# Values and scores of two pairs in one visit of TensorE, and other PSUM banks for the scores

## The chip, the cores and the metric

One NeuronCore of a Trainium2 chip runs the kernel. The metric is the device time of one launch in microseconds, the median of several runs. PE is TensorE's matrix multiplication and PEld its weight load, DVE is VectorE, ACT is ScalarE, POOL is GpSimd, and SP is the engine whose queue issues the DMAs.

## What is computed

Attention with fixed sparsity, and then a two-layer feed-forward block on its output, all in float32:

```
scores = q @ k.T / sqrt(64)                  # 8 batches, 8 heads, 576 positions, 64 wide
heads 0 to 3: key within 32 positions behind the query
heads 4 to 7: key at the same place modulo 32, not after the query
attn = softmax(masked scores);  x = (attn @ v) as 4608 tokens of 512
h = x @ w_in;  g = h * sigmoid(1.702 * h);  out = g @ w_out      # 512 -> 2048 -> 512
```

## The kernel before

**Pairs.** The sparse attention is cut into 42 units that the code calls pairs. Each gathers a few query blocks with the few keys they see: "l" for the local heads, "s" for the strided ones. A pair p goes through these stages, each on its own engine:

- `scores(p)` (L222): small float32 products of 64 rows by 64 columns on PE, into two PSUM banks. A float32 product is two instructions in the trace, so 16 products show as 32.
- `maxima(p)` (L249): DVE adds the mask while it copies the two banks into the buffer `pr` (two SCALAR_TENSOR_TENSOR), then takes the row maxima (`nmax`).
- `softmax(p)` (L282): a generator; ACT makes eight exponentials, two to a step of the generator, then `rinv`; DVE takes its RECIPROCAL; POOL multiplies `pr` by it.
- `transpose(p)` (L309): DVE turns `pr` into `pt_l` or `pt_s` in four steps.
- `values(p)` (L362): PE multiplies `pt` with `v` into two banks `sa`, in 32 products for an "l" pair and 16 for an "s" pair; ACT copies the banks into the token tiles `xl`, `xs`; for the first token blocks DVE then makes a low half (`xl_1`, `xs_1`) from the same banks.

`attend(p)` (L754) is scores, the load of `qk` for pair p+2, maxima, and the start of softmax. Pairs 0 to 4 are done ahead of everything else; the other 37 are laid between the products of the feed-forward block.

**Feed-forward.** The tokens are nine blocks of 512. Every float32 operand is split into a high and a low half (float32r), and a product is three matmuls: high with high, high with low, low with high. Three stages follow each other:

- *Steps.* For blocks 0 to 2, 48 steps of one (block, f): `ffn1(s)` is 12 matmuls of 512 columns into a bank `h`; `act(s)` (L541) is a tanh on ACT and a SCALAR_TENSOR_TENSOR on DVE, both on that bank; `split(s)` makes the halves `gh` (ACT) and `gl` (DVE); `ffn2(s-2)` is 12 matmuls into four banks `o` that stay open for 16 steps. In the first 16 steps the weights are also made ready: per step two items, each two ACT operations on `raw` (`begin_word`, L503), a join on DVE (`raw<-raw`), a high half on ACT (`high`, L481, CAST `w<-raw`) and a low half on DVE (`low`, L493, `w<-raw,w`). The loop is at L981; trace step 9 runs from about 80.8 to 87.5 us.
- *Cycles.* For blocks 3 to 8, two blocks together, eight cycles for each of three rounds (`cycle`, L890): seven products of six matmuls each (a Winograd scheme: a11, s2, a12, s3, a22, s1, s4, banks `ha` and `hs`), and after product i `GAPS[i]` matmuls of the second layer from a queue (`fill`, L847).
- *Tails.* Behind each round of cycles, 16 groups of 12 second-layer matmuls.

**Order.** All engines keep the written order: each queue is first in, first out. The work of pairs is placed by three tables: `turn[p]` is the step in which pair p is transposed, `begin[p]` (L702) the step at whose end its scores are made, and `turn[p] + 2` the step of its values. For the five pairs 5 to 9 (`apart`, L360) `begin` was `turn - 3`; for later pairs it is `turn` of the pair two before, plus 2 or 3.

**Banks.** PSUM has eight banks, shared out by the first letter of a tile's name (L115):

```
def bank(name):
    tag, n = ("s", 2) if name[0] == "s" else ("x", 6)
```

So scores (`s0`, `s1`) and values (`sa0`, `sa1`) take turns in one couple of banks; the six others hold the four `o` and two for `h`, `ha` or `hs`. In a cycle the values of pair p stand in gap 6 (`valued_apart`), and the scores of pair p+2 in gap 0 of the next cycle (`owed`, `attend_ahead`), between two second-layer matmuls each. In the steps the values of pair 10 and later stand between `ffn1(s)` and `ffn2(s-2)`, and the scores of pair p+2 behind that `ffn2`.

Of the kernel before, what the change touches and what calls it, by code (L numbers as in the profile page):

```python
# [42 lines left out]
NF = DFF // P  # L43
# [10 lines left out]
AHEAD = 2  # L54
# [18 lines left out]
}  # L73
GAPS = (4, 4, 4, 3, 3, 3, 3)

# [27 lines left out]
def attn_ffn(ctx, tc, lqk, sqk, lv, sv, w_in, w_out, masks, out):  # L103
# [11 lines left out]
    def bank(name):  # L115
        tag, n = ("s", 2) if name[0] == "s" else ("x", 6)
        return psum.tile([P, 512], F32, tag=tag, name=name, bufs=n)
# [104 lines left out]
    def scores(p):  # L222

        nk, mask = geom(p)
        onto = p < n0
        sps = first[p % 2] if onto else [bank(f"s{j}_{p}") for j in range(2)]
        n = mask.shape[1]
# [119 lines left out]

    xs = {}

    def x_tiles(kind, j):  # L350
# [6 lines left out]
    def x_of(j, c):  # L357
        return (t[:, c % 2, :] for t in x_tiles("l" if c < 2 else "s", j))

    apart = range(n0, n0 + len(windows[0]))  # L360

# [338 lines left out]
    plain = range(n0, p)  # L700
    turn[p] = len(steps) + 2
    begin = {p: turn[p] - 3 for p in turn}  # L702
    for p in turn:
        if p - AHEAD in turn and p not in apart:
            begin[p] = turn[p - AHEAD] + (3 if p - AHEAD in apart else 2)
# [173 lines left out]

    def valued_apart(p):  # L880
        run(values(p))
        load_v(p + 2)

    def attend_ahead(p):
        if p + AHEAD < len(pairs):
            attend(p + AHEAD)

    owed = []

    def cycle(d, c, p, after, start, early):  # L890
# [18 lines left out]
        for i, k in enumerate(order):  # L909
# [47 lines left out]
            if i == 5:  # L957
                eased(HU)
            fill(GAPS[i] // 2)
            if i == 0 and owed:  # L960
                attend_ahead(owed.pop())
            if i == 6 and p is not None:
                valued_apart(p)
                owed.append(p)
            fill(GAPS[i] - GAPS[i] // 2)
        filling.extend(second(a, f + i, (a, f + i)) for i in range(2))
# [14 lines left out]
    for s in range(2, len(steps)):  # L981
# [17 lines left out]
        for k in now:  # L999
            low(k)  # L1000
        for p, t in turn.items():
            if t + 2 == s and p not in apart:
                run(values(p))
                load_v(p + 2)
        act(s)
# [5 lines left out]
        for p, t in turn.items():  # L1011
            if begin[p] < s < t:
                n = t - 1 - begin[p]
                i = s - begin[p]
                run(soft[p], 4 * i // n - 4 * (i - 1) // n)
            if t == s:
                turning[p] = transpose(p)
            if t <= s <= t + 1:
                run(turning[p], 2)
        if s >= LAG and s != NF:  # L1020
            ffn2(s - LAG)
        for p in apart:
            if turn[p] + 2 == s:
                run(values(p))
                load_v(p + 2)
        for p in turn:
            if begin[p] == s:
                attend(p)
        ahead(s)
# [4 lines left out]
    p = plain[-1] + 1  # L1034
    owed.append(plain[-1])
    s1, u2, v5, z = spare
# [7 lines left out]
    for d, (a, b) in enumerate(DOUBLES):  # L1044
# [10 lines left out]
        for c in range(NF // 2):  # L1055
            at = p if 1 <= c <= count else None
            after = p if at is None else p + 1
            after = after if after in soft or at is not None and after < len(pairs) else None
            rest = cycle(d, c, at, after, start, load_gate if c == NF // 2 - 1 else None)
            p += at is not None  # L1060
            start = rest
# [9 lines left out]
        for i in range(NF + 2 if outer else NF):  # L1071
# [3 lines left out]
            for k, q in enumerate(more):  # L1075
# [10 lines left out]
                if at == 3:  # L1086
                    valued_apart(q)
            if not outer:
                prepare(d + 1, i)
            fill(3 * NT)  # L1090
            if i == 0 and owed:
                attend_ahead(owed.pop())
            for k, q in enumerate(more):
                if i - 5 * k - 2 == 3:
                    attend_ahead(q)
        if not outer:
# [101 lines left out]
```

## Time and profile before

| what | value |
| --- | --- |
| median of 3 runs | 866.19 us (865.63 to 867.12) |
| the profiled execution's own time | 867.51 us |
| its span, first to last instruction | 865.7 us |
| PE busy | 853.1 us, 6538 matmuls |
| PEld busy | 682.8 us |
| DVE busy | 556.0 us |
| ACT busy | 440.2 us |
| POOL busy | 200.1 us |
| chain that ended last | PE 88%, DVE 5%, ACT 4% |

Busy shares are means over the whole span. The opening, the steps, the cycles and the tails differ, so what bounds the kernel is read stage by stage, and for PE from the distance between the starts of matmuls, since a busy PE is not yet a PE at its highest rate.

### The profile page before, as it was taken

To read this page: it belongs to the slowest core of one execution; us is meant where nothing else is said; L and a number is where in the kernel's file an instruction comes from. 1 tells how busy PE (TensorE), PEld (TensorE's weight loads), DVE (VectorE), ACT (ScalarE), POOL (GpSimd) and SP (SyncE) were. 2 spreads that over 40 slices of the span, in tenths; PEclk is the share of its full clock that TensorE was granted. 3 is DMA by queue.
4 is the path that set the end of the run, shared out by engine and by line. 5 is a ranking of instruction groups with operands and counts; after the bars stand their busy time and mean duration, and the time that the engine had idled before them with its cause. 6 is when DMAs were issued, how large, how long until landed. Compare 5 with 4: busy or idle time off the path is not lost.

```text
span 865.7 us, 17374 instructions
## 1 busy us (share of the span) xinstructions
PE 853.1 (99%) x6538; PEld 682.8 (79%) x6538; DVE 556.0 (64%) x989; ACT 440.2 (51%) x1330; POOL 200.1 (23%) x177
## 2 busy tenths in 40 slices
PE   9899999999999999999999999999999999999998
PEld 5687778778778877888878778878888888888886
DVE  3789986675576877577668776666766554444522
ACT  6798876544446544545445654545434433332321
POOL 3100104410054600423322012233240012232200
PEclk9999999999999999999999999999999999999999
DMA  9765323882254445676667536666555245455432
GB/s 335 304 243 200 133 64 124 265 258 94 80 168 155 136 141 167 213 211 191 183 189 240 183 116 201 186 182 197 169 160 184 73 161 169 149 166 147 145 123 73
DMA packets 76163, 148.86 MB, mean 172 GB/s; under 512 B 8240, under 2 KB 22960, under 8 KB 76080
## 3 DMA queue, kind: packets, MB, share of 16 engines
q1 hardware_dynamic: 76080, 147.76, 53.3%
q8 instruction: 52, 0.85, 0.4%
q14 instruction: 31, 0.25, 0.1%
HBM read 111.03 MB, written 36.70 MB: 171 GB/s over the span
## 4 chain that ended last, share of the span: by engine, by line
PE 88%; DVE 5%; ACT 4%; DMA 1%; issue 1%; SPq 0%; DVEq 0%; ACTq 0%
PE o L140 43%; PE hs L140 15%; PE h L140 12%; PE ha L140 11%; PE sa L140 3%; PE s L140 3%; DVE raw L140 1%; ACT pr L140 1%; ACT raw L140 1%; DVE w L140 1%; PE t L140 1%; ACT w L140 1%; DVE pt_l L140 1%; DMA raw<-w_out 1%; DVE pt_s L140 1%
## 5 line engine op out<-in xcount | busy, mean ns | idle before, releaser
L140 PE MATMUL o<-w,gh 128*128 128x512 f32 x1152 | 365.7, 393 | 0.3 <-DVE w L140 0.2
L140 PEld LDWEIGHTS o<-w,gh 128*128 128x128 f32 x1152 | 214.6, 188 | 45.5 <-DVE w L140 0.5
L140 PE MATMUL o<-w,gl 128*128 128x512 f32 x576 | 225.6, 392 | 0.0
L140 POOL TENSOR_TENSOR gl<-y,gh 128x512 fp32r<-128x512 f32 x45 | 59.8, 1328 | 301.1 <-ACT gh L140 142.2
L140 PEld LDWEIGHTS o<-w,gl 128*128 128x128 f32 x576 | 108.1, 188 | 22.8
L140 DVE SCALAR_TENSOR_TENSOR y<-tanh,y 128x512 f32<-128x512 f32 x96 | 70.3, 732 | 69.4 <-ACT tanh L140 66.0
L140 POOL TENSOR_TENSOR pr<-pr,rinv 128x432 f32<-128x432 f32 (+1 forms) x42 | 50.1, 1193 | 266.5 <-DVE rinv L140 266.5
L140 ACT ACTIVATE pr<-pr,nmax 128x54 f32<-128x54 f32 (+1 forms) x296 | 101.1, 346 | 5.1 <-DVE nmax L140 4.7
L140 ACT ACTIVATE tanh<-y 128x512 f32<-128x512 f32 x96 | 60.8, 633 | 79.1 <-DVE y L140 78.5
L140 PE MATMUL h<-xl,w 128*128 128x512 f32 x288 | 77.5, 403 | 1.9 <-ACT w L140 1.2
L140 PE MATMUL h<-xs,w 128*128 128x512 f32 x288 | 73.8, 391 | 0.0
L140 DVE TENSOR_TENSOR spare<-hs,spare 128x512 f32<-128x512 f32 x69 | 47.6, 690 | 38.2 <-PE hs L140 37.6
L140 DVE TENSOR_TENSOR gl<-spare,gh 128x512 fp32r<-128x512 f32 x48 | 33.2, 691 | 52.4 <-ACT gh L140 52.1
L140 PEld LDWEIGHTS h<-xl,w 128*128 128x128 f32 x288 | 51.6, 188 | 15.7 <-DVE w L140 2.7
L140 ACT CAST gh<-spare 128x512 fp32r<-128x512 f32 x48 | 29.9, 622 | 65.8 <-PE o L140 63.7
L140 PEld LDWEIGHTS h<-xs,w 128*128 128x128 f32 x288 | 53.8, 188 | 12.0 <-DVE w L140 0.4
L140 DVE STREAM_TRANSPOSE pt_l<-pr 32x256 f32<-32x256 f32 x128 | 55.7, 435 | 2.6 <-POOL pr L140 0.3
L140 DVE SCALAR_TENSOR_TENSOR g<-g,h 128x512 f32<-128x512 f32 x48 | 32.9, 685 | 36.6 <-ACT g L140 36.2
L140 ACT ACTIVATION_READ_ACCUMULATOR pr<-pr,nmax 128x1 f32 x296 | 56.2, 190 | 0.0
L140 DVE STREAM_TRANSPOSE pt_s<-pr 32x256 f32<-32x256 f32 x126 | 54.8, 435 | 2.0
L140 ACT ACTIVATE g<-h 128x512 f32<-128x512 f32 x48 | 29.1, 607 | 51.7 <-PE h L140 32.8
L140 POOL TENSOR_TENSOR y<-spare,spare 128x512 f32<-128x512 f32 x24 | 38.7, 1614 | 30.9 <-issue 28.0
(128 smaller groups left out, 1219.9 us busy)
## 6 DMA issues: line engine op xcount, KB each, us to landing
stream<-s SPq DMA_DIRECT2D x96, 256.0 KB, 2.7
stream<-a SPq DMA_DIRECT2D x72, 256.0 KB, 2.7
gate<-y SPq DMA_DIRECT2D x48, 256.0 KB, 2.3
spare<-gate SPq DMA_DIRECT2D x48, 256.0 KB, 2.8
qk<-sqk SPq DMA_DIRECT2D x23, 452.0 KB, 3.9
qk<-lqk SPq DMA_DIRECT2D x18, 576.0 KB, 4.1
v<-lv SPq DMA_DIRECT2D x18, 512.0 KB, 4.1
out<-out SPq DMA_DIRECT2D x36, 256.0 KB, 2.6
```

What stands on the lines that cost most here:

```text
L140: ins = call(*args, **kw)
```

## The change

Values of pair p and scores of pair p+2 are issued by one function, `visit`: first the value products, then the score products, the load of `qk`, the maxima, and then the copies of the values. Scores of pairs 12 and later get names with "c", which puts them into the six shared banks instead of the couple that the values use; pairs up to 11 keep the couple.

```
-GAPS = (4, 4, 4, 3, 3, 3, 3)
+GAPS = (4, 3, 3, 3, 3, 3, 5)
+FIRST = 1
...
-        sps = first[p % 2] if onto else [bank(f"s{j}_{p}") for j in range(2)]
+        sps = first[p % 2] if onto else [bank(f"{'s' if p - AHEAD in apart or p in apart else 'c'}{j}_{p}") for j in range(2)]
...
     for p in turn:
-        if p - AHEAD in turn and p not in apart:
+        if p - AHEAD in turn:
             begin[p] = turn[p - AHEAD] + (3 if p - AHEAD in apart else 2)
...
+    def visit(before, then):
+        rest = [(p, values(p)) for p in before]
+        for _, x in rest:
+            run(x, 1)
+        for p in then:
+            attend(p)
+        for p, x in rest:
+            run(x)
+            load_v(p + 2)
```

In a cycle the visit stands in gap 6 behind one second-layer matmul, and four follow it:

```
-            fill(GAPS[i] // 2)
-            if i == 0 and owed:
-                attend_ahead(owed.pop())
+            first = FIRST if i == 6 else 0
+            fill(first)
             if i == 6 and p is not None:
-                valued_apart(p)
-                owed.append(p)
-            fill(GAPS[i] - GAPS[i] // 2)
+                seen_to(p)
+            fill(GAPS[i] - first)
```

In a step the visit stands inside `ffn2(s-2)`: behind all of it in the first 16 steps, behind 8 of its 12 matmuls afterwards. The first half of the transposes of a pair (`t == s`) is now issued behind the visit, and it stood ahead of `ffn2` before:

```
+            if t + 1 == s:
+                run(turning[p], 2)
+        behind = second(*steps[s - LAG], s - LAG) if s >= LAG and s != NF else iter(())
+        run(behind, 2 * NT if s > NF else 3 * NT + 1)
+        visit([p for p in turn if turn[p] + 2 == s], [p for p in turn if begin[p] == s])
+        run(behind, 2 * NT)
+        for p, t in turn.items():
             if t == s:
                 turning[p] = transpose(p)
-            if t <= s <= t + 1:
                 run(turning[p], 2)
```

In the tails the scores follow the values without the 12 matmuls that lay between them. By the new `begin`, pairs 7, 8 and 9 have their scores in steps 8, 10 and 12 instead of 6, 8 and 10, one step ahead of their `turn` (9, 11 and 13).

Three places in the order of instructions are shown, before and now.

PE in a cycle, from the last value product of pair 27 on (`sa` is values, `s` and `c` scores of pair 29, `o` second layer, `ha` the product a11). Before:

```order
L140 MATMUL sa_27_4768<-pt_s,v_4408 64x54
L140 MATMUL o_3_4311<-w_1_913,gh_5_4665 128x512
L140 MATMUL o_3_4311<-w_1_913,gl_5_4666 128x512
L140 MATMUL ha_0_4_4793<-b11h,stream_4009 128x512 x4
L140 MATMUL ha_0_4_4793<-b11l,stream_4009 128x512 x2
L140 MATMUL o_0_4262<-w_1_996,gh_6_4708 128x512 x2
L140 MATMUL s_29_4808<-qk_4445 64x54
L140 MATMUL s_29_4809<-qk_4445 64x54
```

Now, where the rows left out are 13 more of the same two kinds of `c_29`:

```order
L141 MATMUL sa_27_4766<-pt_s,v_4430 64x54
L141 MATMUL c_29_4783<-qk_4420 64x54
...
L141 MATMUL c_29_4783<-qk_4420 64x54
L141 MATMUL c_29_4784<-qk_4420 64x54
L141 MATMUL o_2_4291<-w_1_913,gl_5_4666 128x512
L141 MATMUL o_3_4311<-w_1_913,gh_5_4665 128x512 x2
L141 MATMUL o_3_4311<-w_1_913,gl_5_4666 128x512
L141 MATMUL ha_0_4_4817<-b11h,stream_4009 128x512 x4
```

The ten matmuls of 512 columns between values and scores are gone from there, and four stand between the scores and a11.

ACT from step 8 into step 9 (`gh` is the half of step 8's activation, `pr` exponentials, `w` high halves of weights, `g` the tanh of step 9, `xl` the copies of the values of pair 6). Before:

```order
L140 CAST gh_1157<-g_8_1091 128x512
L140 ACTIVATE rinv_1161<-ssum_1015 128x8
L140 CAST w_0_1165<-raw_860 128x512
L140 CAST w_1_1167<-raw_863 128x512
L140 ACTIVATE g_9_1175<-h_1142 128x512
L140 ACTIVATE raw_916<-raw_916 128x512 x2
L140 ACTIVATE raw_919<-raw_919 128x512 x2
L140 ACTIVATE pr_97,ssum_1185<-pr_97,nmax_1138 128x96 x4
L140 CAST xl_0_1236<-sa_6_1202 128x2x4x32
```

Now:

```order
L141 CAST gh_1124<-g_8_1062 128x512
L141 ACTIVATE pr_98,ssum_1128<-pr_98,nmax_1105 128x54 x8
L141 ACTIVATE rinv_1137<-ssum_1128 128x8
L141 CAST w_0_1141<-raw_860 128x512
L141 CAST w_1_1143<-raw_863 128x512
L141 ACTIVATE g_9_1151<-h_1109 128x512
L141 ACTIVATE raw_916<-raw_916 128x512 x2
L141 ACTIVATE raw_919<-raw_919 128x512 x2
L141 CAST xl_0_1204<-sa_6_1170 128x2x4x32
```

All eight exponentials of pair 7 stand ahead of the high halves of the weights, and four of pair 8 are gone from behind the `raw` operations.

DVE at the same place, from the reciprocal on (`w` low halves, `g` step 9's activation, `pt_s` transposes of pair 7, `xl_1` low halves of the values of pair 6, the last row the join of step 10). Before:

```order
L140 RECIPROCAL rinv_1161<-rinv_1161 128x8
L140 TENSOR_TENSOR w_0_1165<-raw_860,w_0_1165 128x512
L140 TENSOR_TENSOR w_1_1167<-raw_863,w_1_1167 128x512
L140 SCALAR_TENSOR_TENSOR g_9_1175<-g_9_1175,h_1142 128x512
L140 STREAM_TRANSPOSE pt_s<-pr_98 32x8x32 x3
L140 TENSOR_TENSOR xl_1_1237<-sa_6_1202,xl_0_1236 128x2x4x32
L140 TENSOR_TENSOR xl_1_1237<-sa_6_1203,xl_0_1236 128x2x4x32
L140 SCALAR_TENSOR_TENSOR raw_916<-raw_916 128x512
```

Now:

```order
L141 RECIPROCAL rinv_1137<-rinv_1137 128x8
L141 TENSOR_TENSOR w_0_1141<-raw_860,w_0_1141 128x512
L141 TENSOR_TENSOR w_1_1143<-raw_863,w_1_1143 128x512
L141 SCALAR_TENSOR_TENSOR g_9_1151<-g_9_1151,h_1109 128x512
L141 TENSOR_TENSOR xl_1_1205<-sa_6_1170,xl_0_1204 128x2x4x32
L141 TENSOR_TENSOR xl_1_1205<-sa_6_1171,xl_0_1204 128x2x4x32
L141 STREAM_TRANSPOSE pt_s<-pr_98 32x8x32 x3
L141 SCALAR_TENSOR_TENSOR raw_916<-raw_916 128x512
```

The low halves of the values now stand ahead of the transposes. The reciprocal stands where it did, but what it waits for on ACT is now eight exponentials and not `rinv` alone.

## Rows read from the trace of the kernel before

**Rows 1.** The page: busy time, share of the span and instructions of each engine.

```profile
PE 853.1 (99%) x6538; PEld 682.8 (79%) x6538; DVE 556.0 (64%) x989; ACT 440.2 (51%) x1330; POOL 200.1 (23%) x177
```

**Rows 2.** Windows: us, busy by engine, granted clock, DMA share, GB/s.

```profile
96.00:106.00 10.00, 10.00 (x74) 7.80 (x73) 9.75 (x19) 9.73 (x33) 1.74 (x1) 1.00 0.30 106
106.00:116.00 10.00, 8.70 (x96) 6.47 (x95) 8.72 (x19) 7.14 (x20) 0.83 (x1) 1.00 0.01 2
130.00:330.00 200.00, 200.00 (x1906) 159.33 (x1906) 136.57 (x262) 102.26 (x386) 63.49 (x63) 1.00 0.49 161
```

**Rows 3.** Waits, 60 to 130 us: us in total, times, longest.

```profile
DVE xl L140 <- ACT xl L140: 1.3, 2, 0.8
PE h L140 <- ACT w L140: 1.2, 2, 1.0
PE h L140 <- DVE w L140: 0.7, 2, 0.3
```

**Rows 4.** Timeline of PE around a visit: start, us, engine, line, operation, tiles, count.

```profile
430.26 0.62 PE L140 MATMUL hs<-b22h,stream 128*128 128x512 f32 x2
430.72 0.61 PE L140 MATMUL hs<-b22l,stream 128*128 128x512 f32 x2
431.17 0.39 PE L140 MATMUL o<-w,gh 128*128 128x512 f32 x1
431.49 0.69 PE L140 MATMUL sa<-pt_s,v 54*64 54x54 f32 x32
432.10 0.50 PE L140 MATMUL o<-w,gh 128*128 128x512 f32 x1
432.44 0.40 PE L140 MATMUL o<-w,gl 128*128 128x512 f32 x1
```

**Rows 5.** The tile sa: durations in ns, least, median, most.

```profile
L140 PE MATMUL sa<-pt_s,v x672: 218/218/258, 73.7 to 632.5; 54*64 54x54 f32 x168
```

**Rows 6.** Timeline of DVE behind s4 of the same cycle.

```profile
431.37 0.69 DVE L140 TENSOR_TENSOR y<-hs,spare 128x512 f32<-128x512 f32 x1 [0.64 <-PE hs L140]
```

**Rows 7.** Timelines of PE and DVE around step 26: second layer, activation.

```profile
194.80 0.62 PE L140 MATMUL o<-w,gh 128*128 128x512 f32 x2
...
195.62 0.69 DVE L140 SCALAR_TENSOR_TENSOR g<-g,h 128x512 f32<-128x512 f32 x1 [1.62 <-ACT g L140]
```

**Rows 8.** Timelines of PE and DVE around the scores of step 19.

```profile
152.70 0.69 PE L140 MATMUL s<-qk 64*64 64x54 f32 x32
...
153.44 0.67 DVE L140 SCALAR_TENSOR_TENSOR pr<-s,masks_sb 128x216 f32<-128x216 f32 x2 [0.39 <-PE s L140]
```

**Rows 9.** Timeline of ACT, steps 8 to 10.

```profile
83.02 0.33 ACT L140 ACTIVATE pr<-pr,nmax 128x54 f32<-128x54 f32 x1
...
83.34 0.33 ACT L140 ACTIVATE pr<-pr,nmax 128x54 f32<-128x54 f32 x1
...
86.25 1.28 ACT L140 CAST w<-raw 128x512 fp32r<-128x512 f32 x2 [1.54 <-DVE raw L140]
87.51 0.60 ACT L140 ACTIVATE g<-h 128x512 f32<-128x512 f32 x1
88.00 2.35 ACT L140 ACTIVATE raw<-raw 128x512 uint32<-128x512 uint8 x4
...
90.61 0.36 ACT L140 ACTIVATE pr<-pr,nmax 128x96 f32<-128x96 f32 x1
...
91.69 0.61 ACT L140 CAST xl<-sa 128x256 fp32r<-128x256 f32 x2
```

**Rows 10.** Timeline of DVE, steps 8 to 10.

```profile
85.53 1.28 DVE L140 SCALAR_TENSOR_TENSOR raw<-raw 128x512 uint32<-128x512 uint32 x2
...
87.33 0.20 DVE L140 RECIPROCAL rinv<-rinv 128x8 f32<-128x8 f32 x1
...
89.33 0.68 DVE L140 SCALAR_TENSOR_TENSOR g<-g,h 128x512 f32<-128x512 f32 x1
...
92.07 0.76 DVE L140 TENSOR_TENSOR xl<-sa,xl 128x256 fp32r<-128x256 f32 x2 [0.82 <-ACT xl L140]
```

**Rows 11.** Timeline of PE, the opening.

```profile
1.00 2.74 PE L140 MATMUL t<-zeros 128*128 128x512 bf16 x6 [1.00 <-DVE zeros L140]
```

More of the change, by code (lines that the diff above doesn't have):

```diff
@@ L348, in attn_ffn @@
     xs = {}
+    apart = range(n0, n0 + len(windows[0]))
     def x_tiles(kind, j):
@@ L358, in x_of @@
         return (t[:, c % 2, :] for t in x_tiles("l" if c < 2 else "s", j))
-    apart = range(n0, n0 + len(windows[0]))
     def values(p):
@@ L700, in attn_ffn @@
     plain = range(n0, p)
-    turn[p] = len(steps) + 2
+    for i in range(AHEAD):
+        turn[p + i] = len(steps) + 2 + 2 * i
     begin = {p: turn[p] - 3 for p in turn}
     for p in turn:
-        if p - AHEAD in turn and p not in apart:
+        if p - AHEAD in turn:
             begin[p] = turn[p - AHEAD] + (3 if p - AHEAD in apart else 2)
@@ L878, in add, with seen_to @@
         vector.tensor_tensor(out=out, in0=a, in1=b, op=ALU.add)
[L880 to L888, printed above, removed]
+    def visit(before, then):
[7 more added lines that the diff above has]
+            load_v(p + 2)
+    def seen_to(p):
+        visit([p], [p + AHEAD] if p + AHEAD < len(pairs) else [])
     def cycle(d, c, p, after, start, early):
@@ L1000, in attn_ffn @@
             low(k)
[L1001 to L1004, printed above, removed]
         act(s)
@@ L1015, in attn_ffn @@
                 run(soft[p], 4 * i // n - 4 * (i - 1) // n)
+            if t + 1 == s:
[5 more added lines that the diff above has]
+        for p, t in turn.items():
             if t == s:
                 turning[p] = transpose(p)
-            if t <= s <= t + 1:
                 run(turning[p], 2)
[L1020 to L1028, printed above, removed]
         ahead(s)
@@ L1034, in attn_ffn @@
     p = plain[-1] + 1
-    owed.append(plain[-1])
     s1, u2, v5, z = spare
@@ L1057, in attn_ffn @@
             after = p if at is None else p + 1
-            after = after if after in soft or at is not None and after < len(pairs) else None
+            after = after if after in soft else None
             rest = cycle(d, c, at, after, start, load_gate if c == NF // 2 - 1 else None)
@@ L1086, in attn_ffn @@
                 if at == 3:
-                    valued_apart(q)
+                    seen_to(q)
             if not outer:
@@ L1090, in attn_ffn @@
             fill(3 * NT)
[L1091 to L1095, printed above, removed]
         if not outer:
```

## Prediction

> **What bounds the kernel now.** I read the page first: PE is busy 853.1 of 865.7 us [rows 1]. Busy is not peak rate, so the next view is PE's timeline. From 430.26 to 431.17 four matmuls of 512 columns start [rows 4], one in 0.227 us, and this is the distance nearly everywhere outside the small products. The windows then give the stages. From 130 to 330 us PE is busy 200.00 of 200 us at a granted clock of 1.00 [rows 2]: it waits for nothing, so whatever PE itself issues there is on the path. From 96 to 106 us DVE is busy 9.75 and ACT 9.73 of 10, and from 106 to 116 PE only 8.70 [rows 2]. The waits say for what: products h wait for weight halves, 1.2 us for ACT's and 0.7 for DVE's [rows 3]. So there are two bounds. Up to some 130 us, where weights are made ready, the pair of ACT and DVE sets the pace; behind that PE does.
>
> **The merged visits (gain).** What does leaving the wide matmuls for small ones cost? Around values of an "s" pair, second-layer matmuls start at 431.17 and 432.44 with one more and 32 small ones between [rows 4]. Without the small ones that would be two distances, 0.455 us; the visit costs 1.27 - 0.455 = 0.82. The 32 are busy 0.69 and the last of them lasts 0.22 [rows 5], so their starts spread over 0.47, and with one more distance of 0.015 they use 0.48. The other 0.335 is the change from wide to small and back: 0.09 on entry (431.49 - 431.17 - 0.227), 0.11 on the second wide matmul (432.44 - 432.10 - 0.227), the rest between the last small and the first wide one. Scores are of the same form, 64*64 [rows 8], and as busy, 0.69, so I take the same entry and exit for them. The change puts 30 scores, those of pairs 12 to 41, straight behind the values of pairs 10 to 39: 30 entries and exits go, 30 x 0.335 = 10.05 us, all beyond 130 us and on PE's path. No row shows values and scores side by side. The bounds are 0, if the junction costs as much as an exit and an entry, and 10.05, if it costs nothing. I take 10.05: inside a visit the products already change their operands and banks every 0.015 us.
>
> The Trainium skill, "TensorEngine Tiling (Array Packing)", section "Tiling Modes", Key Properties, says that TensorE is drained when the tiling mode changes and not when only the tile does. Values and scores both work in tiles of 64 by 64, so by it the junction is free; no row here shows that.
>
> **Waits of the scores for their new banks (loss).** One of the two banks was the last to be read. In a cycle that reader is DVE's add behind s4, from 431.37 to 432.06 [rows 6]. The scores would come 0.47 + 0.015 behind the first value product at 431.49, at 431.98, so they wait some 0.15 us with the signal's way. Values of an "l" pair have twice the instructions and cover it. Of the 12 merged visits in cycles 5 have "s" values: 0.75 us. In a step the reader is the activation: DVE ends it at 196.31, 1.51 us behind the first second-layer matmul [rows 7], and the scores come 8 x 0.227 + 0.09 + 0.485 = 2.39 behind it. Nothing, except in a step in which ACT also rounds a sum of weights (seven steps), say 0.35 in all (estimate). Together 1.1; bounds 0 and 3.
>
> **Waits for the score banks (nothing).** The next wide product needs the bank that DVE empties first. The scores' last start is at 152.70 + 0.47 = 153.17, DVE begins at 153.44 and two copies take 0.67 [rows 8], so the first is done some 0.6 us behind that start. Four second-layer matmuls lie between, 0.13 + 0.11 + 4 x 0.227 = 1.15 us. If that cover were gone, each visit would pay up to 0.6. For the wide "l" scores, if the product took the other bank, it would wait 0.1 to 0.2 in some dozen visits: this is in the upper bound of 3.
>
> **Gaps, queues.** After s2 and a12 one second-layer matmul less follows, after s4 two more. A product's bank is used again two products later, at least 12 starts or 2.7 us on; the reader needs 0.69 and begins within 0.64 us of DVE's wait [rows 6]. Nothing; without that cover 0.23 a piece. On SP the loads of `qk` and `v` now stand together behind a visit instead of half a step apart; each is for two pairs later, over 10 us on. Nothing.
>
> **The early stage (loss).** Here DVE and ACT are full, and the change puts one behind the other. Pairs 7, 8 and 9 get their scores one step before their transposes, so in steps 9, 11 and 13 all eight exponentials stand between the maxima and the high halves of the weights. One takes 0.32 us at width 54 (83.02 to 83.34), 0.36 at width 96 (90.61 to 91.69 is three) [rows 9]: 2.6 or 2.9 us. With 0.1 to start and 0.2 for `rinv`, DVE reaches the reciprocal 2.9 or 3.2 us after the maxima; before it, DVE has 1.8 us of joins and halves (85.53 to 87.33 [rows 10]). It idles 1.1, 1.4 and 1.1. Then its low halves wait for a high half of 0.65 that started with the reciprocal (pair of them 1.28 [rows 9]): 0.35 each. Sum 4.65.
>
> In the same steps DVE's low halves of the values now stand ahead of the transposes, and wait for ACT's copies, which stand behind 2.25 us of `raw` operations (88.00 to 90.25, overlap counted) and take 0.37 for the first. Before, the transposes filled that time. Against the activation's end (89.33 + 0.68 [rows 10]) carried along with the new delays, the wait is 1.2 in step 9, 0.4 in step 11 and 1.7 in step 13: 3.3. Before it was 1.3 in all [rows 3, 10], which goes. So DVE loses 4.65 + 3.3 - 1.3 = 6.7 us, and as PE already waits for these halves [rows 3], PE loses it too; nothing later gives it back, since PE is at its full rate there. Bounds: 3, if the maxima that leave the way (pair 8's, 2.0 us, and pair 9's, 1.3) give DVE a lead that holds; 10, if each copy wait is its full 1.8 and no idle time of before falls away.
>
> **Sum.** -10.05 + 1.1 + 6.7 = -2.25 us. Against the profiled execution's own 867.5 us (span 865.7) that is 865.3. The median of the runs shown, 866.2, lies 1.3 below that execution; the forecast for the median is **863.9 us**.
>
> **Rivals.**
> *A, the early stage hardly suffers.* DVE's lead holds and the stage loses 3: -10.05 + 1.1 + 3 = -5.95, 860.2 us. For it: DVE's maxima move two steps later. Against: DVE has no idle time in which to build a lead [rows 2].
> *B, the junction is not free.* Scores are other operands with other waits than values, so an entry and exit may remain in part. Half of it is 5.0 us: -5.0 + 1.1 + 6.7 = +2.8, 869.0 us, slower. It decides the sign from (10.05 - 7.8) / 30 = 0.075 us a junction. For it: nothing in the trace shows such a junction. Against: 0.015 us from product to product inside a visit.
> *C, TensorE's clock falls.* In steps 11 and 13 PE would stand still for about 2.4 us each time before h. In this trace the longest such wait is 1.0 [rows 3] and the granted clock stays at 1.00 [rows 2], so it shows no fall. At the lower level six wide matmuls took 2.74 us in the opening, about 0.45 each [rows 11], 0.22 more than now; a dozen of them after each hole are 2 x 2.7 = 5.4 us: +3.1, 869.3 us. The Trainium skill, "TensorE: Matmul & The Clock Gate", section "HAM oscillation — how this bites in real kernels", has the rule that a TensorE left idle between bursts is set back to half rate; no run here shows it for holes of this size.
> *D, no net change.* The junction or the bank waits take 2 us more than in the sum: within 0.2%.
>
> **From cases to numbers.** My forecast, both large terms within about 2 us of the sum, has 0.52. A has 0.20, B 0.10, C 0.05, D 0.13. A measurement of this kernel tells 0.2% from no change, 1.7 us. The forecast's own spread, 861.5 to 866, lies beyond 864.5 for a bit over six parts in ten: 0.33 of its 0.52 is faster and 0.19 the same. Faster: 0.33 + 0.20 + 0.02 of D = 0.55. Same: 0.19 + 0.08 of D = 0.27. Slower: B, C and 0.03 of D = 0.18. The range 859.5 to 868 leaves out the lower half of A and most of B and C, some 0.2; the forecast's own is 861.5 to 866.
>
> **What would show it.** Right: beyond 130 us visits of values and scores with starts 0.02 us apart at the junction, and a merged visit 0.33 us cheaper than the two; in cycles 0.1 to 0.2 of wait at the first scores behind "s" values; the stage up to h of step 16 some 6 to 7 us later, with DVE idle before the reciprocals and before the low halves of the values, and PE waiting over 2 us for ACT's or DVE's w in steps 11 and 13. Wrong: a gap at the junction; PE waits for score banks; a granted clock below 1.00; or an early stage that is hardly longer.

## The result, and the profile of the changed kernel

The changed kernel takes 871.68 us, the median of 7 runs (870.86 to 873.36), against 866.19 us of 7 runs of the kernel before (865.63 to 869.57): the ratio of the means is 1.0059, 95% interval 1.0045 to 1.0074. It is 0.6% slower. The forecast, 863.9 us with a range of 859.5 to 868, was wrong in size and in sign.

The profiled execution took 871.68 us itself (span 869.9). Its page, to be read against [rows 1]:

```profile
PE 851.6 (98%) x6538; PEld 690.9 (79%) x6538; DVE 557.0 (64%) x989; ACT 440.5 (51%) x1330; POOL 200.4 (23%) x177
...
PEclk9899899999999999999999999999999999999999
```

TensorE (PE) is busy 1.5 us less in a span 4.2 us longer, and in two of the forty slices the granted clock is under nine tenths of full, where it was above that in all forty before. The windows of [rows 2], now:

```profile
96.00:106.00 10.00, 7.64 (x59) 5.71 (x60) 8.00 (x14) 8.10 (x27) 1.47 (x1) 0.97 0.16 48
106.00:116.00 10.00, 10.00 (x68) 7.92 (x67) 8.40 (x19) 6.28 (x15) 0.00 (x0) 0.86 0.38 127
130.00:330.00 200.00, 196.14 (x1894) 158.97 (x1894) 136.24 (x262) 104.87 (x389) 62.82 (x63) 0.99 0.48 153
```

VectorE (DVE) and ScalarE (ACT), nearly full from 96 to 106 us before, now stand idle there a fifth of the time, and from 130 to 330 us TensorE, which never stopped before, lacks 3.9 us. The waits from 60 to 130 us say for what the first part waits, against [rows 3]:

```profile
PE h L141 <- ACT w L141: 4.2, 3, 1.6
DVE rinv L141 <- ACT rinv L141: 4.1, 3, 1.5
...
DVE xl L141 <- ACT xl L141: 2.8, 2, 1.7
DVE w L141 <- ACT w L141: 2.5, 5, 0.7
...
PE h L141 <- DVE w L141: 2.3, 3, 1.1
...
```

To find where the 4.2 us came in, the span is cut at four starts in TensorE's timeline: the first product of h in step 3, that of step 16, and the first product behind the steps (`ha`). In the kernel before they are:

```profile
44.33 1.65 PE L140 MATMUL h<-xl,w 128*128 128x512 f32 x6
...
131.89 1.52 PE L140 MATMUL h<-xl,w 128*128 128x512 f32 x6
...
332.65 0.84 PE L140 MATMUL ha<-b11h,stream 128*128 128x512 f32 x3
```

And in the changed one:

```profile
42.94 1.65 PE L141 MATMUL h<-xl,w 128*128 128x512 f32 x6
...
139.99 0.84 PE L141 MATMUL h<-xl,w 128*128 128x512 f32 x3
...
342.93 0.85 PE L141 MATMUL ha<-b11h,stream 128*128 128x512 f32 x3
```

The fourth cut is the start of the last matmul, 861.40 before and 865.62 now. So the opening is 1.39 us shorter, the **early stage** (step 3 to step 16) 97.05 us in place of 87.56 (+9.49), the **steps** from 16 on 202.94 in place of 200.76 (+2.18), and the **cycles** and what follows 522.69 in place of 528.75 (-6.06): +4.22 together. The opening differs from execution to execution (its end lay between 42.0 and 46.4 us over all profiles of this study, those with the order of before included), and the early stage does not depend on it: it took 97.05 us after openings that ended at 42.94, 44.23 and 44.52 us. So the stretches are compared, and the opening is left out.

Two merged visits show what the change gained. Around 488 us nothing waits:

```profile
488.24 0.39 PE L141 MATMUL o<-w,gl 128*128 128x512 f32 x1
488.56 0.69 PE L141 MATMUL sa<-pt_s,v 54*64 54x54 f32 x32
489.06 0.65 PE L141 MATMUL c<-qk 64*64 64x54 f32 x32
489.64 0.73 PE L141 MATMUL o<-w,gh 128*128 128x512 f32 x2
490.21 0.39 PE L141 MATMUL o<-w,gl 128*128 128x512 f32 x1
```

The scores `c` start 0.50 us behind the values, of which 31 distances of 0.015 are 0.47: the junction costs 0.03. From 488.24 to 490.21 is 1.97 us, less three wide distances of 0.227 it is 1.29, where two separate visits cost 1.64 [rows 4]: 0.35 is saved. In the cycles with "s" values the scores wait for DVE's add, as forecast:

```profile
405.48 0.69 PE L141 MATMUL sa<-pt_s,v 54*64 54x54 f32 x32
405.98 0.80 PE L141 MATMUL c<-qk 64*64 64x54 f32 x32
406.71 0.50 PE L141 MATMUL o<-w,gl 128*128 128x512 f32 x1
```

From the first value to the next wide matmul it is 1.23 us here and 1.08 above: 0.15 of wait, in five cycles. The loss in the steps is another matter. Step 41, first on TensorE:

```profile
297.66 0.61 PE L141 MATMUL o<-w,gh 128*128 128x512 f32 x2
...
299.56 1.14 PE L141 MATMUL sa<-pt_l,v 64*64 64x32 f32 x64
300.52 0.29 PE L141 MATMUL c<-qk 64*64 64x54 f32 x2
302.93 0.77 PE L141 MATMUL c<-qk 64*64 64x54 f32 x30 [2.12 <-DVE g L141]
303.63 0.80 PE L141 MATMUL o<-w,gl 128*128 128x512 f32 x1
```

The scores have two of the six shared banks. The first is free, the second is still read by the activation of the same step, and the visit stops for 2.4 us (300.54 to 302.93). ACT and DVE in that time:

```profile
294.36 0.60 ACT L141 ACTIVATE g<-h 128x512 f32<-128x512 f32 x1 [4.28 <-DVE gl L141]
294.85 0.33 ACT L141 ACTIVATE pr<-pr,nmax 128x54 f32<-128x54 f32 x1
...
297.44 1.03 ACT L141 CAST b11h<-xl 128x1024 fp32r<-128x1024 f32 x1
298.38 1.05 ACT L141 CAST plain<-summed 128x1024 fp32r<-128x1024 f32 x1
299.33 0.61 ACT L141 CAST gh<-g 128x512 fp32r<-128x512 f32 x1
...
301.56 0.60 ACT L141 ACTIVATE g<-h 128x512 f32<-128x512 f32 x1 [1.51 <-DVE gl L141]
```

```profile
298.50 1.23 DVE L141 TENSOR_TENSOR b11l<-xl,b11h 128x1024 fp32r<-128x1024 f32 x1 [0.99 <-ACT b11h L141]
299.65 1.22 DVE L141 TENSOR_TENSOR summed<-summed,plain 128x1024 fp32r<-128x1024 f32 x1
300.78 0.68 DVE L141 TENSOR_TENSOR gl<-g,gh 128x512 fp32r<-128x512 f32 x1
...
302.19 0.69 DVE L141 SCALAR_TENSOR_TENSOR g<-g,h 128x512 f32<-128x512 f32 x1 [0.61 <-ACT g L141]
```

In step 40 ACT has eight exponentials (294.85 to 297.44), then rounds `b11` and a sum of weights (1.03 and 1.05 us), DVE takes their low halves (1.23 and 1.22), and only then `gl` of step 40. `g` has one buffer, so the tanh of step 41 waits for `gl`, 1.51 us, and DVE's second half of the activation ends at 302.88. This is what the scores wait for. Worked out in the same way from TensorE's timeline, the waits are 1.02 us in step 23, 0.88 in 35, 0.41 in 37, 0.43 in 39 and 2.4 in 41: 5.1 in all. In the other steps there is none. Behind the wait of step 41 the granted clock falls to the lower of its two levels (1.2 of 2.4 GHz):

```profile
300.00:310.00 10.00, 7.88 (x101) 6.40 (x95) 5.81 (x12) 2.73 (x9) 6.69 (x7) 0.83 0.56 179
```

### The profile page after: what moved, and what is told of

Read it like the earlier page. It is cut to its first block, busy times and chain, and to the rows that moved or that the text cites. A ratio compares the mean times of both kernels' runs of the same rounds, so it can differ in the third digit from the quotient of the medians.

```text
span 869.9 us, 17299 instructions
## 1 busy us (share of the span) xinstructions
PE 851.6 (98%) x6538; PEld 690.9 (79%) x6538; DVE 557.0 (64%) x989; ACT 440.5 (51%) x1330; POOL 200.4 (23%) x177
## 4 chain that ended last, share of the span: by engine, by line
PE 81%; ACT 8%; DVE 8%; issue 2%; DMA 0%; SPq 0%; ACTq 0%; DVEq 0%
PE o L141 39%; PE hs L141 15%; PE ha L141 11%; PE h L141 9%; ACT pr L141 4%; PE sa L141 2%; PE c L141 2%; DVE pt_l L141 2%; ACT raw L141 1%; DVE gl L141 1%; ACT g L141 1%; ACT w L141 1%; DVE pr L141 1%; PE t L141 1%; DVE w L141 1%
## 5 line engine op out<-in xcount | busy, mean ns | idle before, releaser
L141 PE MATMUL o<-w,gh 128*128 128x512 f32 x1152 | 379.6, 390 | 0.4 <-DVE w L141 0.2
L141 PE MATMUL o<-w,gl 128*128 128x512 f32 x576 | 228.1, 396 | 0.0
L141 POOL TENSOR_TENSOR gl<-y,gh 128x512 fp32r<-128x512 f32 x45 | 62.0, 1378 | 293.3 <-PE ha L141 149.8
L141 DVE SCALAR_TENSOR_TENSOR y<-tanh,y 128x512 f32<-128x512 f32 x96 | 67.9, 708 | 55.3 <-ACT tanh L141 53.0
L141 PE MATMUL h<-xs,w 128*128 128x512 f32 x288 | 76.2, 401 | 0.0
L141 PEld LDWEIGHTS h<-xl,w 128*128 128x128 f32 x288 | 54.7, 195 | 20.7 <-ACT w L141 4.6
L141 PEld LDWEIGHTS h<-xs,w 128*128 128x128 f32 x288 | 56.5, 197 | 12.4
L141 ACT COPY spare<-ha 128x512 f32<-128x512 f32 x24 | 14.1, 587 | 71.5 <-PE ha L141 71.5
```

Of the source, the lines that this page charges most:

```text
L141: ins = call(*args, **kw)
```

## The experiments

Theory T1: the early stage is longer because ACT and DVE take turns there. T2: in the steps the scores wait for an activation that the rounding of sums makes late. T3: a merge gains one entry and exit. R1 to R3 are the rivals that the expectations name. All eighteen kernels, with the stretches of each one's profiled execution (us). Each ratio is one of means, to runs of the kernel before taken alongside, whose medians lay between 866.19 and 867.30 us; so ratios are compared, and differences of medians of about 1 us between kernels say nothing.

| kernel | median | ratio to before (95%) | early stage | steps | cycles on |
|---|---|---|---|---|---|
| before | 866.19 | | 87.56 | 200.76 | 528.75 |
| changed | 871.68 | 1.0059 (1.0045 to 1.0074) | 97.05 | 202.94 | 522.69 |
| e1_begin | 869.58 | 1.0024 (1.0011 to 1.0038) | 93.56 | 201.43 | 523.76 |
| e2_turns | 868.16 | 1.0011 (0.9998 to 1.0024) | 92.96 | 201.08 | 522.65 |
| e3_both | 863.61 | 0.9961 (0.9944 to 0.9978) | 87.58 | 204.26 | 522.66 |
| e6_fill | 872.43 | 1.0073 (1.0054 to 1.0092) | 97.78 | 203.12 | 522.66 |
| e4_sums | 873.04 | 1.0065 (1.0048 to 1.0082) | 97.88 | 201.28 | 522.70 |
| e5_all | 862.92 | 0.9957 (0.9942 to 0.9973) | 87.58 | 202.56 | 522.66 |
| e7_split | 877.13 | 1.0118 (1.0099 to 1.0136) | 97.05 | 203.03 | 526.75 |
| e8_first | 872.83 | 1.0065 (1.0045 to 1.0084) | 97.05 | 203.15 | 522.03 |
| e9_nosums | 867.81 | 1.0011 (0.9995 to 1.0027) | 96.91 | 197.28 | 523.12 |
| e10_apart | 873.04 | 1.0068 (1.0047 to 1.0088) | 97.00 | 204.16 | 523.26 |
| e11_best | 862.33 | 0.9950 (0.9933 to 0.9968) | 87.54 | 204.25 | 522.06 |
| e12_control | 876.50 | 1.0115 (1.0091 to 1.0138) | 87.56 | 210.48 | 528.75 |
| e13_spaced | 879.30 | 1.0144 (1.0117 to 1.0172) | 96.99 | 208.79 | 523.00 |
| e14_best | 867.05 | 1.0004 (0.9989 to 1.0019) | 87.56 | 207.30 | 523.16 |
| e15_mixed | 867.47 | 1.0014 (1.0000 to 1.0028) | 96.89 | 197.73 | 522.65 |
| e16_best | 857.45 | 0.9889 (0.9871 to 0.9906) | 87.59 | 197.57 | 522.05 |

### The early stage: e1_begin, e2_turns, e3_both, e6_fill

e1_begin:

```diff
-        if p - AHEAD in turn:
+        if p - AHEAD in turn and p not in apart:
```

> The scores of pairs 7, 8 and 9 begin in steps 6, 8 and 10 again, as before the change, so that their eight exponentials are spread over the step in between. Theory T1 (the early stage is longer because ScalarE and VectorE now take turns): the three VectorE waits ahead of the reciprocals (1.26, 1.54 and 1.27 us in the changed kernel's trace) go, so h of step 16 starts about 4 us earlier than the 139.99 us of the changed kernel, and the time is 867 to 868 us. Rival R1 (the fall of TensorE's granted clock to half in front of steps 10, 12 and 14 costs the stage): the values still stand alone in front of h there and h still waits for weights, so the stage changes by under 1.5 us and the time is 870 to 872 us.

The stage fell by 3.49 us, near the 4 expected and against R1, which allowed 1.5; the median fell by 2.1 only, to 869.58, above T1's range. The profiled execution took 867.66, so part of the gap is the spread of its runs (867.52 to 871.86).

e2_turns, in the loop over steps (the block behind the visit stays, for `s > NF`):

```diff
                 run(turning[p], 2)
+            if t == s and s <= NF:
+                turning[p] = transpose(p)
+                run(turning[p], 2)
         behind = ...
```

> In the first sixteen steps the transposes of a pair whose turn it is go back in front of the visit. T1: the VectorE waits ahead of the low halves of values (1.08, 0.71 and 1.70 us) shrink because the transposes run while ScalarE makes the high halves; h of step 16 starts 2 to 3.5 us earlier, and the time is 868 to 870 us. If those waits only move elsewhere: no change, 871 to 872 us.

The stage fell by 4.09 us, a little more than expected, and the median to 868.16.

e3_both has both edits.

> Both edits of e1_begin and e2_turns: the first sixteen steps have the order of before, but for the values, which stand with the scores. T1: h of step 16 starts within 1 us of the 131.89 us of the kernel before, and the time is 863 to 865 us, below the kernel before by 1 to 3 us. If the waits add in another way than T1 has it: 866 to 869 us.

The stage is back at 87.58 us, the 87.56 of before, and the median is 863.61. The waits from 60 to 130 us are again those of [rows 3], and no row for the reciprocals is left:

```profile
DVE xl L141 <- ACT xl L141: 1.2, 2, 0.8
PE h L141 <- ACT w L141: 1.1, 2, 1.0
...
PE h L141 <- DVE w L141: 0.6, 2, 0.3
```

So two moves made the whole loss: the scores of pairs 7 to 9 two steps later, and the transposes behind the visit. Taken back singly they give 3.5 and 4.1 us, together 9.5: they do not simply add. Values directly in front of scores play no part here, since no visit ahead of step 16 has both, in any of these kernels.

The steps behind this stage show what a fall of the clock costs there. e1_begin waits in the visits of the same steps as the changed kernel, and as long to 0.1 us, but from 290 to 310 us the granted clock is 1.00 where the changed kernel has 0.91: its steps are 1.5 us shorter. e3_both has these waits too and a clock of 0.83, and its steps are 2.8 us longer than e1_begin's. So this fall differs from execution to execution, and it is paid.

e6_fill leaves the order of the changed kernel alone and keeps TensorE at work in part of the holes ahead of h:

```diff
             hps[s] = bank(f"h_{s}")
+            for _ in range(6 if s in (10, 12, 14) else 0):
+                matmul(hps[s]..., lhsT=zeros, rhs=zeros..., start=True, stop=True)
```

> Six more matmuls of zeros (128x512) stand in front of the first product of h in steps 10, 12 and 14, where TensorE idles 1.3 to 1.65 us and its granted clock then falls; they write zeros that h's first product overwrites. T1 (VectorE and ScalarE set the pace there, TensorE waits anyway): the clock falls go, h of step 16 moves by under 0.7 us, and the time is 871 to 872.5 us. R1 (the clock falls cost the stage): h of step 16 starts 3 to 5 us earlier, and the time is 866.5 to 868.5 us.

The window from 80 to 130 us in the changed kernel (the granted clock is the third number from the end):

```profile
80.00:130.00 50.00, 43.52 (x397) 33.28 (x396) 39.39 (x76) 35.40 (x104) 3.30 (x3) 0.90 0.30 101
```

And with the fill:

```profile
80.00:130.00 50.00, 43.86 (x415) 31.06 (x413) 39.53 (x75) 35.01 (x103) 3.29 (x3) 1.00 0.32 104
```

The falls of the clock behind the holes of steps 10, 12 and 14 are gone, and the stage is not shorter, 97.78. One came in step 15 instead: 0.76 from 130 to 137 us. That one has a price. In e4_sums (below), whose order in this stage is the changed kernel's, the clock fell there too (0.76), and in both kernels step 15 took 11.3 to 11.4 us and the stage 97.8 to 97.9; in e9_nosums and e15_mixed the clock was 1.00 there, step 15 took 10.4 and the stage 96.9. The falls behind steps 10, 12 and 14 cost next to nothing: e8_first had two of the three, and 97.05 us like the changed kernel. R1, which gave these three 3 to 5 us, falls: there TensorE waits for ACT and DVE anyway.

### The junction and the bank of the cycles: e7_split, e8_first

e7_split:

```diff
-    def visit(before, then):
+    def visit(before, then, between=lambda: None):
         rest = [(p, values(p)) for p in before]
         for _, x in rest:
             run(x, 1)
+        between()
...
-        visit([p], [p + AHEAD] if p + AHEAD < len(pairs) else [])
+        visit([p], [p + AHEAD] if p + AHEAD < len(pairs) else [], lambda: fill(1))
...
-            fill(GAPS[i] - first)
+            fill(GAPS[i] - first - (i == 6 and p is not None))
```

> In the fifteen merged visits behind the steps one wide matmul of those that stood behind the visit stands between the values and the scores. Theory T3 (a visit costs 0.335 us for going in and coming out, and the junction of values and scores nothing): 15 x 0.335 = +5.0 us, less five waits of 0.154 us for the bank behind the seventh product (0.77 us), which the wide matmul covers: +4.2 us, 875 to 877 us. Rival R3 (what a split costs is the start of the scores' own weights, not the change between wide and narrow matmuls; the merge gains nothing): 870.5 to 872 us.

The stretch of the cycles grew by 4.06 us (4.2 expected); the median, 877.13, is 0.1 above T3's range. T3 holds and R3 falls: what a merge gains is the entry and the exit. The split in the trace:

```profile
491.92 0.69 PE L141 MATMUL sa<-pt_s,v 54*64 54x54 f32 x32
492.54 0.49 PE L141 MATMUL o<-w,gh 128*128 128x512 f32 x1
492.96 0.28 PE L141 MATMUL c<-qk 64*64 64x54 f32 x4
```

From values to scores it is now 1.04 us, against 0.50 in the merged visit: 0.54, of which the wide matmul itself is 0.227.

e8_first has `FIRST = 2`.

> Two wide matmuls in place of one stand between the seventh product of a cycle and the visit, and three in place of four behind it. The five waits of 0.154 us for the bank behind the seventh product go: -0.8 us, 870.5 to 871.3 us. If the wait moves behind the visit, to the next cycle's first product: 871.5 to 872 us.

The cycles became 0.66 us shorter and the scores start without a wait (0.51 behind the values):

```profile
407.33 0.69 PE L141 MATMUL sa<-pt_s,v 54*64 54x54 f32 x32
407.84 0.65 PE L141 MATMUL c<-qk 64*64 64x54 f32 x32
```

The median, 872.83, is above both ranges and does not show it: the spread of the runs (870.41 to 874.50) is larger than 0.7 us. The trace carries the finding, the time does not.

### The waits in the steps: e4_sums, e5_all, e9_nosums, e10_apart to e16_best

e4_sums:

```diff
-SUMS = (17, 19, 21, 33, 35, 37, 39, 41)
+SUMS = (18, 20, 22, 34, 36, 38, 40, 42)
```

> The eight sums of weights are each taken one step later (18, 20, 22, 34, 36, 38, 40, 42 in place of 17, 19, 21, 33, 35, 37, 39, 41), so that ScalarE rounds them in a step behind a visit and not in the step ahead of one. Theory T2 (the scores wait for the second activation of their own step, which is late because ScalarE and VectorE rounded sums in the step before): the five waits inside the visits of steps 23, 35, 37, 39 and 41 (together 5.2 us) go, with them the fall of the clock in step 41; the first sixteen steps stay as they are, and the time is 865 to 866.5 us. Rival R2 (the waits come from the exponentials of the softmax and would be there without the sums): 870.5 to 872.5 us.

A miss for T2 and for R2. The steps fell by 1.66 us only, and the median did not. By the timeline the waits went in steps 35 and 37, but 0.91 us stayed in step 23, 0.55 in 39 and 3.0 in 41, and new ones of 0.27 came in 25 and 45. The rows of steps 39 and 40 say why, DVE's and then ACT's tanh of step 40:

```profile
292.94 1.75 DVE L141 TENSOR_TENSOR summed<-summed,plain 128x1024 fp32r<-128x1024 f32 x1
294.61 1.22 DVE L141 TENSOR_TENSOR gl<-g,gh 128x512 fp32r<-128x512 f32 x1
```

```profile
295.93 0.60 ACT L141 ACTIVATE g<-h 128x512 f32<-128x512 f32 x1 [5.44 <-DVE gl L141]
```

The sum is rounded behind the visit now, but its low half still stands ahead of a `gl`, that `gl` ahead of the next tanh (one buffer), and the tanh ahead of the eight exponentials. The lateness is carried into step 41. T2 had to be widened: it is enough that DVE is late in the odd step before.

e5_all adds e3_both's edits.

> The edits of e3_both and e4_sums together. T1 and T2 add: e3_both's 863.6 us less 5.5 to 6.5 us, 856.5 to 859 us, below both kernels, with no wait over 0.2 us inside a visit of the steps 17 to 47. If the sums' lateness only shows once the early stage is short: 860 to 863 us.

862.92 us, above its range for the same reason; its early stage is 87.58 us. The time lies in the second range, but not by what that range stood for: e4_sums has these waits behind a long early stage too.

e9_nosums takes the suspected work away:

```diff
-        scalar.copy(out=plain_w[c].bitcast(F32R), in_=summed[c])
+        pass
...
-        vector.tensor_tensor(out=s.bitcast(F32R), in0=s, in1=a, op=ALU.subtract)
```

> The rounding of the sums of weights is left out altogether (ScalarE's copy and VectorE's subtraction of each of the eight sums; the sums go to memory as they stand, so the products behind the steps use other halves). T2 as e4_sums leaves it (any rounding in the step ahead of a visit, or in the odd step before that, makes the activation of the visit's step late, by way of the one buffer of the activation's output and of ScalarE's eight exponentials): the waits of 1.02, 0.88, 0.41 and 0.43 us in steps 23, 35, 37 and 39 go, the one of step 41 falls from about 2.6 us to 1 to 1.6 us, since the rounding of b21 and b11 stays; from h of step 16 to the first product behind the steps 197.5 to 199.5 us in place of 202.94, and the time is 866 to 868.5 us. R2 (the exponentials alone make the waits): 870.5 to 872.5 us.

As T2 has it, or a little better: 867.81 us, 197.28 us for the steps, no wait in steps 23 to 39, and in step 41 one of 1.0 us, with the rounding of `b11` still ahead of it:

```profile
300.04 0.68 PE L141 MATMUL c<-qk 64*64 64x54 f32 x30 [0.67 <-DVE g L141]
```

R2 falls: the exponentials are all there.

e10_apart keeps all the work and spreads it. Its core:

```diff
-SUMS = (17, 19, 21, 33, 35, 37, 39, 41)
+SUMS = (18, 20, 22, 30, 34, 38, 40, 42)
...
-    -9: [("b21", "+")], -8: [("b11", "+")], -6: [("t1", "-")], -5: [("t1", "+")],
+    -15: [("b21", "h")], -14: [("b21", "l")], -11: [("b11", "h")], -10: [("b11", "l")], -6: [("t1", "-")], -5: [("t1", "+")],
...
             if at == 1:
                 high_sums(c)
+            if at == 2:
                 low_sums(c)
```

> All the rounding stays, but no step has two of them: ScalarE rounds a sum in an odd step behind the visit, VectorE takes its low half in the even step after, and b21 and b11 are rounded in the same way in steps 33 and 34, 37 and 38 in place of 39 and 40. T2: no wait over 0.4 us inside a visit, no fall of the clock in step 41; from h of step 16 to the first product behind the steps 197 to 199 us in place of 202.94, and the time is 865 to 867.5 us. R2: 870.5 to 872.5 us.

From step 27 to step 43 no scores wait, step 41 included:

```profile
305.40 0.67 PE L141 MATMUL c<-qk 64*64 64x54 f32 x32
```

But the steps took 204.16 us: the visit of step 23 waited 1.4 us, that of step 25, which had no wait before, 3.9, and behind it the granted clock fell to the lower level (0.79 in the mean from 194 to 206 us). GpSimd (POOL) stood in front of the third sum until the one before it was written to memory, and the softmax's product for DVE's transposes was behind it in its queue:

```profile
188.36 1.43 POOL L141 TENSOR_TENSOR summed<-plain 128x256 f32<-128x256 f32 x2 [9.67 <-DMA s<-plain]
```

> The edits of e3_both, e10_apart and e8_first together. T1, T2 and the bank behind the seventh product add: e3_both's 863.6 us less 4 to 6.5 us and less 0.7 us: 856.5 to 859.5 us, some 1% below the kernel before.

e11_best, the edits of e3_both and e8_first with these, has the same stall (its visit of step 25 waits 3.9 us): 862.33 us, above its range.

> The edits of e10_apart in the kernel before, where scores have banks of their own and wait for no activation. T2: the rounding was late there for nobody, 865.5 to 867 us, no change. If the rounding cost the kernel before as well: 861 to 864 us.

e12_control has the edits of e10_apart in the kernel before. Its time says nothing on its own, 876.50 us, for the same stall of POOL. From step 33 on it answers the question: from h of step 35 to that of 36, and from 37 to 38, it takes 7.65 us each, as in the kernel before, while e10_apart shortened the same two distances of the changed kernel from 8.30 and 7.82 to 7.43 each. In these steps the rounding delays nobody where the scores do not take the activation's banks.

e13_spaced has `SUMS = (18, 22, 28, 32, 36, 40, 42, 44)`, and e14_best e3_both's and e8_first's edits with it.

> As e10_apart, but the first sums begin four and six steps apart (18, 22, 28, 32, 36, 40, 42, 44), so that GpSimd does not find the tiles of the sum before still being written to memory; b21 is rounded in steps 35 and 36, b11 in 39 and 40. T2: no wait over 0.4 us inside a visit and no stall of GpSimd; from h of step 16 to the first product behind the steps 196.5 to 198.5 us in place of the changed kernel's 202.94, and the time is 865 to 867.5 us. If the sums cannot be placed without a stall elsewhere: 869 us or more.

> The edits of e3_both, e13_spaced and e8_first together: e11_best's 862.3 us less the stall of GpSimd in steps 24 and 25, its steps falling from 204.25 us to 196.5 to 198.5 us: 855.5 to 858 us, 1% below the kernel before.

Both missed, at 879.30 and 867.05 us: no scores waited over 0.3 us up to step 29, but now POOL stood in front of the third sum for a tile that products of h still read, and the visit of step 45 had a new wait of 1.2 us:

```profile
POOL summed L141 <- PE h L141: 18.5, 1, 18.5
```

e15_mixed leaves the first three sums where the changed kernel has them and takes the rest from e10_apart (`SUMS = (17, 19, 21, 30, 34, 38, 40, 42)`, low halves one step on for the first three); e16_best adds the edits of e3_both and e8_first.

> The first three sums stay where the changed kernel has them (17, 19, 21, both halves in the step after), the other five and b21 and b11 stand as in e10_apart, where they made neither waits nor a stall. T2: the wait of 1.02 us in step 23 stays, those of steps 35, 37, 39 and 41 go with the fall of the clock; from h of step 16 to the first product behind the steps 197 to 198.5 us in place of 202.94, and the time is 866 to 868 us. If a stall turns up elsewhere again: 869 us or more.

> The edits of e3_both, e15_mixed and e8_first together: e3_both's 863.6 us less 4 to 6.5 us and less 0.7 us, 856.5 to 859.5 us, about 1% below the kernel before.

Both came out as expected: 867.47 us with 197.73 us for the steps, and 857.45 us, 1.1% below the kernel before. In e16_best h of step 16 starts here:

```profile
132.00 1.29 PE L141 MATMUL h<-xl,w 128*128 128x512 f32 x5
```

From there to the last matmul it takes 719.6 us where the kernel before takes 729.5: 9.9 us less. This is the gain of the merged visits, with the waits of the change taken away but for 1.3 us. The moved roundings can hardly have added to it, since TensorE waited for nothing in the steps of the kernel before [rows 2].

## Why the prediction was wrong

**The merged visits: right.** -10.05 us was forecast at 0.335 a piece. All visits from step 16 on cost 61.2 us in the kernel before, by TensorE's timeline, and 52.1 in e16_best; without its two waits in steps 23 and 45 (1.0 and 0.3 us) that is 10.4 less for 30 merges, 0.346 each. The Trainium skill, "TensorEngine Tiling (Array Packing)", section "Tiling Modes", Key Properties, has the drain at a change of the tiling mode only, and the trace agrees: 0.03 us at the junction, 0.32 (e7_split: 4.06 and the 0.77 of covered waits, over 15) to 0.35 for an entry with its exit. Rival B falls.

**The bank behind s4: right.** 5 x 0.15 was forecast and 5 x 0.15 is in the trace; e8_first takes it away.

**The banks in the steps: the step that failed.** The prediction took the reader's end from step 26, 1.51 us behind the first second-layer matmul against scores at 2.39 [rows 7], and allowed 0.35 us for the steps in which ACT also rounds a sum. Step 26 is a step without rounding, and has none in the step ahead. Where a sum, `b21` or `b11` is rounded in the step ahead, the same activation ends up to 5.2 us behind it (297.66 to 302.88 in step 41): there are eight exponentials and 2.1 us of rounding on ACT, 2.45 on DVE, with `gl` behind these and the tanh behind `gl`. In place of 0.35 there were 5.1 us of waits, above the bound of 3 that the prediction gave for all the scores' waits, and a fall of the granted clock in step 41: 0.83 from 300 to 310 us. The price of that fall is 1.5 us: so much shorter are the steps of e1_begin, with the same waits and a clock of 1.00. Two more runs agree: e4_sums, whose waits in the steps are still 5.0 us, the clock there 1.00 and the steps 1.7 us shorter; and e15_mixed, which shortens the steps by 5.2 us, of which the waits of steps 35 to 41 are 4.1, less 0.4 that steps 23 and 45 wait more, so that some 1.5 are left for the clock. The prediction looked at the engine that frees the bank and not at what stands ahead of it in two engines' queues.

**The early stage: mechanism right, size short.** Forecast 6.7 us with bounds of 3 and 10, measured 9.5. Ahead of the reciprocals 1.1, 1.4 and 1.1 us were forecast, 4.1 in all are in the waits; for the copies 3.3 less 1.3, and DVE's waits for `xl` and `xs` over the whole stage rose from 2.3 to 5.1; for the low halves of weights 1.05, and they rose from 2.1 to 3.2. DVE's waits grew by 8.4 us in all. The rest of the 9.5 is work that lasted longer: DVE's busy time in the stage is 80.34 us against 79.03. e3_both shows that nothing else is in it. Rival A falls.

**The clock: rival C came true and cost next to nothing where it was looked for.** TensorE stood still before h of steps 10, 12 and 14, for 1.2 to 1.6 us and again for 0.6 to 1.1 two matmuls later, 2.0 to 2.4 in each step, and the granted clock fell three times. The prediction had two such holes, of about 2.4 us, and priced their falls at 5.4 us, by 0.45 us a matmul in the opening. The granted clock reads 1.00 there (0 to 4 us), so these rows do not show the lower level; the changed kernel bears the 0.45 out, where four matmuls of h take from 88.29 to 90.14 us, 0.46 each, at the lower level (granted clock 0.51 from 88.3 to 91.7 us):

```profile
88.29 2.06 PE L141 MATMUL h<-xl,w 128*128 128x512 f32 x4 [0.57 <-DVE w L141]
90.14 2.29 PE L141 MATMUL h<-xs,w 128*128 128x512 f32 x6
```

What the prediction had wrong is that a slower TensorE delays anything there: e6_fill and e8_first show these falls all but free. Step 41 shows a fall that is paid, where TensorE is the bound, and step 15 one of 0.9 us. The Trainium skill, "TensorE: Matmul & The Clock Gate", section "HAM oscillation — how this bites in real kernels", has a TensorE that is left idle between bursts fall back to half rate; the trace agrees for these three holes, which stand behind small products, and not for every one: in e8_first the hole of step 14 is as long, and in e4_sums TensorE waits 3 us in step 41, both at a clock of 1.00.

**The sum with the measured terms.** -10.4 for the merges, +0.8 behind s4, +5.1 and +1.5 in the steps, +9.5 in the early stage: +6.5, against +5.6 in the three stretches. Of the 0.9 us between them some 0.7 lie just outside the visits: the second to eleventh distances between wide matmuls behind a visit are a few ns longer than 0.227 us, which makes 1.9 us for the 63 visits of the kernel before and 1.2 for the 33 of e15_mixed. The rest is not placed. So the merges gain some 11 us in all, a little more than forecast.

## What to carry to other kernels

When work takes over a bank that another engine frees, read that reader's end in the worst step, not in a plain one: list what stands ahead of it in its own queue and in the queue of the engine that feeds it, two steps back. A saving on the bounding engine is kept only if the helper engines' order stays as it was where they are the bound; here the same merge is worth +0.6% or -1.1% of the time, by where some roundings, exponentials and transposes stand in the helpers' queues. Stops of TensorE and falls of its clock cost time only where TensorE is the bound: 1.5 us in step 41, next to nothing in steps 10, 12 and 14.

## What was not expected of the hardware

The same subtraction on DVE does not always last the same. `gl` takes 0.68 us at 300.78 in the changed kernel and 1.22 at 294.61 in e4_sums; the low half of a sum takes 1.22 us at 299.65 and 1.75 at 292.94. In both long cases POOL was adding weights at the time, in both short ones it was not, and POOL was slowed too: its addition took 1.72 us at 291.88 in e4_sums, beside DVE's rounding, and 0.74 at 189.74 in e10_apart, where DVE stood idle. No run was made to take this apart, but all eighteen traces sort the same way. Of their `gl` operations the 1671 beside which POOL was idle took 0.68 to 0.70 us, and the 111 that overlap a POOL instruction 0.68 to 1.65; of the low halves of sums, 126 without overlap took 1.22 to 1.23 us, and the ten with it 1.32 to 1.90. And matmuls of zeros kept the granted clock at 1.00 through holes in which it fell without them; that it then fell at the next hole, in step 15, is not shown to be their doing, since it fell there in e4_sums too.
